# Loading only the non-zero halves of a filter's tables, with interleaved columns, for the first batch

## The chip, the cores and the metric

The kernel runs on one core of a Trainium2 chip. The metric is device time in microseconds, the median of several runs. The engines are named as in the profile: PE (TensorE matmul), PEld (its weight loads), DVE (VectorE), ACT (ScalarE), POOL (GpSimd) and SP (SyncE, which here only issues DMAs).

## The reference

Eight batches of 3008 x 256 float32 go through a spectral filter along the sequence (an FFT, a product with a complex filter, an inverse FFT), and the result through an MLP mixer over tokens and channels.

```python
X = np.fft.rfft(x, axis=1)                       # x: (8, 3008, 256)
Y = X * (filt_r + 1j * filt_i)[None]             # filters: (1505, 256)
x = np.fft.irfft(Y, n=3008, axis=1).astype(np.float32)

h = np.maximum(x.transpose(0, 2, 1) @ w_tok1, 0.0) @ w_tok2     # 3008 -> 256 -> 3008
u = x + h.transpose(0, 2, 1)
h2 = np.maximum(u @ w_ch1, 0.0) @ w_ch2                         # 256 -> 1536 -> 256
return (u + h2).astype(np.float32)
```

## The kernel before

The length 3008 is split as 47 x 64, and the Fourier transforms are written as matmuls with tables: first one of length 64 (`a_unit`), then one of length 47 (`b_unit`), the product with the filter on DVE, then the inverse of length 47 (`bi_unit`). The inverse of length 64 is folded into the mixer. The batches go through the filter in groups (0), (1, 2), (3, 4), (5, 6), (7). The first group, batch 0, has code of its own inside `dft` (`first` is true): its intermediate values stay on chip, transposed by DVE in the tile `turned`, and nothing else can run on PE but the conversion of the mixer's weights, which are stored in 64 bits and are rebuilt as float32 meanwhile. From the second group on, the filter's steps are slotted between the mixer's matmuls of earlier batches.

For the first batch the loop runs over k = 0 to 31. Step k does `b_unit(k)` (a matmul of 128x128 by 128x256 on L617, then a DVE product on L622) and `bi_unit(k - 1)` (two accumulating matmuls with 96 columns of weights on L631, then an ACT copy on L641). Two steps form a pair, which shares one table tile and one filter tile. Once a pair:

- `table_load` (L559) loads the table of the pair four ahead, by SP. It has the forward table (128 columns) and the inverse one (96 columns) for both steps of the pair: 128 rows of 2 x 224 floats. The tiles come from the pools `wbp` (three buffers) and `t1p` (two) in turn, so that five tables are on chip at once.
- `filt_load` (L225 to L232) loads the filter rows of the pair four ahead, by POOL, in six DMAs.
- `filt_double` (L237) and `table_turn` (L244, L245) copy on ACT: the filter's rows to the other half of the partitions, and the inverse table with its halves exchanged and one of them negated, into `turn_i`.
- the pair's results are written to DRAM by an ACT DMA (L638), and read back later into the `t4` tiles (L726).
- a tile of w_tok1 (by SP, L332) or w_tok2 (by POOL, L347) is loaded and converted (ACT L265, DVE L267 to L273, PE L311 and L312, ACT L314).

The tables have zeros. In the stored form their rows stand for four kinds of values; rows 0 to 63 reach only forward columns 0 to 63 and inverse columns 0 to 47, and rows 64 to 127 only the other columns. The kernel before loads the zeros too.

The order of the work on each engine is the order of the calls in the code (a manual schedule). Within a step of k the kernel calls `b_unit(k)`, then, on even k, `filt_load` and `table_load`, then `bi_unit(k - 1)`, and on odd k `filt_double` and `table_turn` for the next pair; the conversions follow at the end of the step. After the loop the first token sums (L732) start, and then the mixer.

Of the kernel before, what the change touches and what calls it, by code (L numbers as in the profile page):

```python
# [10 lines left out]
FP32 = mybir.dt.float32  # L11
# [12 lines left out]
P = 128  # L24
K2 = 32
A = 24
KR = 4 * A
KH = KR // 2
HALF = 64
# [5 lines left out]
XF = 2 * FB  # L35
KC = 2
WC = 2
DT = 256
TC = DT // P
DC = 1536  # L40
# [15 lines left out]
def _make_tables():  # L56
    n2 = np.arange(N2)
    one, two = slice(0, HALF), slice(HALF, P)
    wa = np.zeros((P, K2, 4))
    wai = np.zeros((K2, 4, P))  # L60
    for k2 in range(K2):
        th, th1 = (2 * np.pi * ((n * k2) % N2) / N2 for n in (n2, n2 + 1))
        c, s, c1, s1 = np.cos(th), np.sin(th), np.cos(th1), np.sin(th1)
        alt, alt1 = 1.0 - 2.0 * (n2 % 2), 2.0 * (n2 % 2) - 1.0
        rows = ((c, c1), (-s, s1), (-s, -s1), (c, -c1)) if k2 else ((c, c1), (alt, alt1), (c, -c1), (alt, -alt1))
        for g, (plus, minus) in enumerate(rows):
            wa[one, k2, g], wa[two, k2, g] = plus, minus
        wai[k2] = wa[:, k2].T * (2.0 if k2 else 1.0)
    wa, wai = wa.reshape(P, P), wai.reshape(P, P)

    n1 = A - 1 - np.arange(A)
    wb = np.zeros((4, A, K2, P))
    wi = np.zeros((P, K2, 4, A))
    for k2 in range(K2):
        for s in range(2 * A):
            if s < A:
                k, sign, q = k2 + 64 * s, 1.0, s
            else:
                j = s - A + 1
                k, sign, q = 64 * j - (k2 if k2 else 32), -1.0, 32 + s - A  # L80
                if j == A and k2:
                    continue
            th = 2 * np.pi * ((n1 * k) % N) / N
            c, sn = np.cos(th), np.sin(th)
            edge = k in (0, NF - 1)
            if edge:
                sn = np.zeros(A)
            if k2:
                parts = ((0, q, c), (1, q, sign * sn), (2, HALF + q, sign * c), (3, HALF + q, -sn))
            else:  # L90
                parts = ((s // A, q, c), (2 + s // A, HALF + q, -sn))
            for g, to, w in parts:
                wb[g, :, k2, to] = w * np.where(n1 == 0, 0.5, 1.0)
                wi[to, k2, g] = w * (1.0 if k2 or edge else 2.0) / N
    f = np.float32
    wi = wi.reshape(P, K2, KR)
    wa0 = wa.reshape(P, K2, 4).transpose(0, 2, 1).reshape(P, P)
    wbi0 = np.zeros((4, K2, K2, P + KR))
    wbi0[:, 0:A, :, 0:P] = wb
    wbi0 = wbi0.reshape(P, K2, P + KR)  # L100
    wbi0[:, :, P:] = wi
    wb = wb.reshape(KR, K2, P)
    wbi = np.zeros((P, K2 // KC, 4, HALF))
    for h in range(2):
        r, to = slice(h * HALF, h * HALF + KH), slice(h * HALF, (h + 1) * HALF)
        for i in range(KC):
            wbi[r, :, i] = wb[h * KH:(h + 1) * KH, i::KC, to]
            wbi[i * HALF:(i + 1) * HALF, :, 2 + h, 0:KH] = wi[to, i::KC, h * KH:(h + 1) * KH]
    wa = wa.reshape(P, K2, 4)
    by_sum = np.zeros((P, 2, 2, K2))  # L110
    for e in range(2):
        for h in range(2):
            by_sum[:, e, h, 0] = wa[:, 0, 2 * e + h]
            by_sum[:, e, h, 1:] = wa[:, 1:, 2 * h + e]
    wa = by_sum.reshape(P, P)
    return wa.astype(f), np.concatenate((wa[one], wa[one])).astype(f), wa0.astype(f), wai.astype(f), wbi.astype(f), wbi0.astype(f)
# [3 lines left out]
def kernel(  # L120
# [11 lines left out]
    nc = tc.nc  # L132
# [7 lines left out]
    wbi_d = nc.inline_tensor(wbi_np, name="wbi_t").ap()  # L140
    wa0_d = nc.inline_tensor(wa0_np, name="wa0_t").ap()
    wbi0_d = nc.inline_tensor(wbi0_np, name="wbi0_t").ap()
# [8 lines left out]
    def pool(name, bufs, **kw):  # L151
        return ctx.enter_context(tc.tile_pool(name=name, bufs=bufs, **kw))
# [3 lines left out]
    t1p = pool("t1p", 2)  # L156
    wbp = pool("wbp", 3)
# [15 lines left out]
    def bank(tag):  # L173
        return (psg if tag == "pg" else psum).tile([P, 512], FP32, tag=tag, name="ps_" + tag)
# [5 lines left out]
    def free_bank():  # L180
        turn.reverse()
        return turn[0]
# [10 lines left out]
    filts_0 = list(filts)  # L193
    w1 = glob.tile([P, A, DT], FP32, name="w1")

# [4 lines left out]
    turned = wcp.tile([P, K2 * D + P], FP32, tag="wc", name="turned")  # L200
    wa0 = turned[:, K2 * D:]
    turned = turned[:, 0:K2 * D].rearrange("p (s d) -> p s d", d=D)
# [32 lines left out]
    def filt_double(c):  # L235
        t = filts_0[c % len(filts_0)]
        nc.scalar.copy(out=t[HALF:P], in_=t[0:HALF])  # L237


    turn_i = sp.tile([P, 4, WC, KR], FP32, tag="s", name="turn_i")  # L240

    def table_turn(g, wb):
        wi, to = wb[:, :, P:], turn_i[:, g % 4]
        nc.scalar.copy(out=to[0:HALF], in_=wi[HALF:P])  # L244
        nc.scalar.activation(out=to[HALF:P], in_=wi[0:HALF], func=AF.Copy, scale=-1.0)  # L245

# [71 lines left out]
    def w1_load(i):  # L318
# [6 lines left out]
        for h in range(2):  # L325
# [3 lines left out]
            if h == 0:  # L329
                src = bass.AP(tensor=rows.tensor, offset=rows.offset + (A - 1 - lo) * DT,  # L330
                              ap=[[N1 * DT, N2], [-DT, n], [1, DT]])
            q.dma_start(st[h * HALF:(h + 1) * HALF, 0:n * DT].rearrange("p (a t) -> p a t", t=DT), src)  # L332
        yield
# [180 lines left out]
    def half_of(half, n=HALF):  # L514
        return slice(half * HALF, half * HALF + n)
# [30 lines left out]
    def dft(bs):  # L546
        first = bs[0] == 0
        nb = len(bs)
        tiled = bs not in GROUPS[0:2]
        todo = [(b, c) for b in bs for c in range(NXC // 2 if tiled else NXC)]  # L550
        wbs = {}

        def table_load(c):
            if c * KC % WC == 0:
                g = c * KC // WC
                where, tag = (t1p, "t1") if first and g % 5 > 2 else (wbp, "wb")
                shape, src = ([P, WC, P + KR], wbi0_d[:, ts(g, WC), :]) if first else ([P, 4, HALF], wbi_d[:, g])
                wbs[g] = where.tile(shape, FP32, tag=tag, name="wb")
                nc.sync.dma_start(wbs[g], src)  # L559

        def w_load(c):
            table_load(c)
# [51 lines left out]

        def b_unit(k):
            ps = bank("pg").rearrange("p (b d) -> p b d", b=2)[:, 0:nb, :]
            nc.tensor.matmul(ps, wbs[k // WC][:, k % WC, 0:P], turned[:, k, :].unsqueeze(1), start=True, stop=True)  # L617
            t = filts_0[k // KC % len(filts_0)]
            if k == 0:
                prods["all"] = p1p.tile([P, 2, 2, D], FP32, tag="p1", name="p1")  # L620
            p1 = prods["all"][:, k % 2]
            nc.vector.tensor_tensor(out=p1, in0=ps.to_broadcast([P, 2, D]), in1=t[:, :, k % KC, :], op=ALU.mult)  # L622
            prods[k] = (p1[:, 0:1], p1[:, 1:2])

        def bi_unit(k):


            ps = bank(free_bank()).rearrange("p (b d) -> p b d", b=2)[:, 0:nb, :]
            for i, p in enumerate(prods.pop(k)):
                wi = turn_i[:, k // WC % 4, k % WC] if i else wbs[k // WC][:, k % WC, P:]  # L630
                nc.tensor.matmul(ps[0:KR], wi, p, start=(i == 0), stop=(i == 1))  # L631
            c, r = divmod(k, KC)
            if r == 0:
                where, tag = (p2p, "p2") if c % 3 == 2 else (t3p, "t3")
                t3s[c] = where.tile([KR, KC, nb, D], FP32, tag=tag, name="t3")
            by_block(t3s[c][:, r], ps[0:KR])
            if r == KC - 1:
                nc.scalar.dma_start(g_d[0][ts(c, KC)].rearrange("k r b d -> r k b d"), t3s.pop(c))  # L638

        def by_block(out, ps):  # L640
            nc.scalar.copy(out=out.rearrange("p b (e g i) -> p b g e i", e=DH, i=CW),  # L641
                           in_=ps.rearrange("p b (g e i) -> p b g e i", e=DH, i=CW))
# [52 lines left out]
        if first:  # L695
            for i in range(2):
                t = t2p.tile([P, 2, KC, D], FP32, tag="t2", name="filt")
# [6 lines left out]
        for k in range(K2 + 1):  # L704
            if k < K2:
                b_unit(k)
                if first and k % KC == 0:
                    if k // KC + 4 < K2 // KC:
                        filt_load(k // KC + 4)
                    if k // KC + 4 < K2 // KC:  # L710
                        table_load(k // KC + 4)
            if k >= 1:
                bi_unit(k - 1)
            if first and k % KC == KC - 1 and k + 1 < K2:
                filt_double(k // KC + 1)
                table_turn(k // KC + 1, wbs[k // KC + 1])
            yield
# [338 lines left out]
    with tc.manual_schedule():  # L1056
# [6 lines left out]
        for i, _ in enumerate(dft(GROUPS[0])):  # L1063
            if i == 0:
                nc.scalar.dma_start(wai_t, wait_d)
            k = i - NXC - 2
# [113 lines left out]
```

## Time and profile before

| | |
|---|---|
| time, median of 3 runs | 2464.59 us (2463.82 to 2464.80) |
| the profiled execution's own time | 2465.54 us |
| its span, first to last instruction | 2463.4 us |
| PE busy | 2414.3 us, 98% of the span |
| DVE, ACT, POOL busy | 75%, 28%, 24% |
| DMA | 236.07 MB, of which 16 table loads of 224 KB for the first batch |
| loop over k of the first batch | 31.28 to 109.55 us of the span |
| granted clock of PE, mean | 0.994 |

All times inside the execution are counted from the start of the span. In a line of instructions in order of time, the first number is the start, the second the time taken (for several instructions, from the first start to the last end), and what stands in brackets is the idle time before it and what ended that. In a line of waits, the numbers are the total, how many times, and the longest.

### The profile page before, as it was taken

The numbers are of one execution on the slowest core, as the hardware profiler recorded it, in microseconds if no ns is written. First come the engines' busy times: TensorE is split into PE (matmuls) and PEld (weight loads), VectorE is DVE, ScalarE is ACT, GpSimd is POOL, SyncE is SP. The second block draws the span as 40 slices with busy tenths as digits, with TensorE's granted clock in tenths as the row PEclk, the third lists the DMA queues.
The fourth block names the chain that finished last, engine by engine and source line by source line (L and its number), as shares of the span: only waits on it lengthen the run. The fifth ranks groups of instructions, "written<-read, shape, count | busy, mean of one in ns | idle before, by whom it ended". The sixth has DMA issues, their size and how long they took to land.

```text
span 2463.4 us, 33933 instructions
## 1 busy us (share of the span) xinstructions
PE 2414.3 (98%) x11836; PEld 1962.0 (80%) x11836; DVE 1843.2 (75%) x3404; ACT 679.4 (28%) x1348; POOL 594.1 (24%) x1081
## 2 busy tenths in 40 slices
PE   7899999999999999999999999999999999999998
PEld 3566676978878887887888878897888888898887
DVE  7787778587885888578875887857786788757776
ACT  5633222133221222123221222213221222212222
POOL 6573332112111211211221112112212112112121
PEclk8999999999999999999999999999999999999999
DMA  9974434353431321235332322323322121201100
GB/s 214 254 223 134 140 112 139 103 156 115 119 88 49 86 84 56 90 109 167 101 84 69 86 73 79 103 57 116 98 66 73 50 71 46 97 24 29 40 14 20
DMA packets 173586, 236.07 MB, mean 96 GB/s; under 512 B 33757, under 2 KB 123563, under 8 KB 173416
## 3 DMA queue, kind: packets, MB, share of 16 engines
q1 hardware_dynamic: 128600, 175.59, 24.3%
q0 software_dynamic: 33216, 48.32, 7.9%
q10 hardware_dynamic: 11600, 10.00, 1.3%
q8 instruction: 94, 1.54, 0.3%
q14 instruction: 76, 0.62, 0.1%
HBM read 156.56 MB, written 77.22 MB: 95 GB/s over the span
## 4 chain that ended last, share of the span: by engine, by line
PE 88%; DVE 7%; DMA 2%; issue 1%; ACT 1%; POOL 0%; DVEq 0%; SPq 0%; ACTq 0%; POOLq 0%
PE ps_po L889 33%; PE ps_pg L855 18%; PE ps_pg L871 14%; PE ps_b L732 3%; PE ps_acc L732 3%; PE ps_b L512 3%; PE ps_b L776 3%; PE ps_acc L776 2%; PE ps_acc L512 2%; PE ps_b L754 2%; PE ps_acc L754 2%; DVE t L833 1%; DVE hh L833 1%; DMA filt<-in_filt_i_dram 1%; DVE u L833 1%
## 5 line engine op out<-in xcount | busy, mean ns | idle before, releaser
L936 POOL DMA_DIRECT2D out_dram<-r x752 | 408.1, 551 | 1645.3 <-ACT hh L876 1467.3
L833 DVE TENSOR_TENSOR hh<-ps_pg,s 128x512 f32<-128x512 f32 (+3 forms) x864 | 482.6, 586 | 383.9 <-ACT s L858 379.7
L876 ACT ACTIVATE hh<-hh 128x512 f32<-128x512 f32 (+1 forms) x576 | 348.0, 621 | 958.4 <-DVE hh L833 956.4
L889 PE MATMUL ps_po<-t,wc 128*128 128x256 f32 (+1 forms) x2304 | 546.4, 380 | 4.6 <-DVE t L833 3.5
L889 PEld LDWEIGHTS ps_po<-t,wc 128*128 128x128 f32 x2304 | 426.6, 190 | 129.5 <-DVE t L833 43.0
L889 PE MATMUL ps_po<-hh,wc 128*128 128x256 f32 (+1 forms) x1728 | 414.2, 375 | 1.3 <-POOL wc L371 0.8
L855 PE MATMUL ps_pg<-v,wc 128*128 128x256 f32 (+1 forms) x1728 | 414.7, 376 | 0.0
L889 PEld LDWEIGHTS ps_po<-hh,wc 128*128 128x128 f32 x1728 | 326.8, 190 | 42.9 <-ACT s L858 3.9
L855 PEld LDWEIGHTS ps_pg<-v,wc 128*128 128x128 f32 x1728 | 327.7, 190 | 40.4 <-DVE v L833 2.6
L871 PE MATMUL ps_pg<-u,wc 128*128 128x256 f32 (+1 forms) x1152 | 295.1, 379 | 0.5 <-DVE hh L833 0.5
L871 PEld LDWEIGHTS ps_pg<-u,wc 128*128 128x128 f32 x1152 | 215.0, 190 | 57.1 <-DVE hh L833 23.5
L833 DVE TENSOR_TENSOR t<-t,hh 128x256 f32<-128x256 f32 (+1 forms) x576 | 245.0, 425 | 19.9
L833 DVE TENSOR_TENSOR s<-ps_pg,hh 128x512 f32<-128x512 f32 (+1 forms) x288 | 196.1, 681 | 31.4 <-DVE hh L833 1.8
L858 ACT COPY s<-ps_pg 128x256 f32<-128x256 f32 (+1 forms) x288 | 106.0, 368 | 331.4 <-PE ps_pg L855 328.4
L833 DVE TENSOR_TENSOR t<-hh 128x512 f32<-128x512 f32 (+1 forms) x288 | 193.2, 671 | 0.6 <-ACT hh L876 0.6
L855 PE MATMUL ps_pg<-u,wc 128*128 128x256 f32 (+1 forms) x576 | 171.7, 380 | 2.6 <-DVE hh L833 2.6
L871 PE MATMUL ps_pg<-v,wc 128*128 128x256 f32 (+1 forms) x576 | 168.8, 375 | 0.0
L855 PEld LDWEIGHTS ps_pg<-u,wc 128*128 128x128 f32 x576 | 106.8, 190 | 34.3 <-DVE hh L833 18.9
L871 PEld LDWEIGHTS ps_pg<-v,wc 128*128 128x128 f32 x576 | 109.2, 190 | 12.6
L833 DVE TENSOR_TENSOR u<-ps_b,u 128x256 f32<-128x256 f32 (+2 forms) x102 | 58.3, 572 | 67.3 <-PE ps_b L776 61.8
L833 DVE TENSOR_TENSOR u<-ps_acc,u 128x512 f32<-128x512 f32 (+2 forms) x108 | 62.4, 577 | 55.8 <-PE ps_acc L776 51.5
L732 PE MATMUL ps_b<-t,w 128*128 128x256 f32 x384 | 86.3, 388 | 4.0 <-issue 4.0
(134 smaller groups left out, 2460.3 us busy)
## 6 DMA issues: line engine op xcount, KB each, us to landing
w<-w_tmp SPq DMA_DIRECT2D x35, 896.0 KB
out_dram<-r POOLq DMA_DIRECT2D x696, 32.0 KB, 2.4
t<-g_tmp SPq DMA_DIRECT2D x42, 512.0 KB
g_tmp<-t SPq DMA_DIRECT2D x96, 192.0 KB
t<-z_tmp SPq DMA_DIRECT2D x180, 96.0 KB
z_tmp<-t SPq DMA_DIRECT2D x60, 256.0 KB
filt<-in_x_dram SPq DMA_DIRECT2D x90, 128.0 KB
wb<-wbi_t SPq DMA_DIRECT2D x64, 128.0 KB
```

What stands on the lines that cost most here:

```text
L512: nc.tensor.matmul(outs(i, j), stat(i, j), mov(i, j), start=True, stop=True)
L732: nc.tensor.matmul(acc[:, t, :], w1[:, a, ts(t, P)], t4[b, a // TC4][:, a % TC4, :], start=(a == 0 and t == 0), stop=(a == A - 1 and t == ...
L754: nc.tensor.matmul(ps[:, ds(q * P, n)], t4[b, c][:, r, ts(dh, P)], wai[:, 0:n], start=(first and q == 0), stop=(not first and q == 3))
L776: nc.tensor.matmul(ps[:, ds(j * hw, hw)], h1[:, n, :], w2m[m % 2][:, at, 0:hw], start=(i < 2 and j == 0), stop=(j == len(todo) - 1))
L833: nc.vector.tensor_tensor(out=out, in0=in0, in1=in1, op=op)
L855: nc.tensor.matmul(ps[:, 0:hw], chan[0][:, jp, n, :], mov, start=True, stop=True)
L858: nc.scalar.copy(out=s[:, 0], in_=g[0][:, 0, 0:hw])
L871: nc.tensor.matmul(ps[:, 0:hw], chan[0][:, jp, n, :], mov, start=True, stop=True)
L876: nc.scalar.activation(out=hs, in_=hs, func=AF.Relu)
L889: nc.tensor.matmul(po[i][:, j, 0:hw], chan[1][:, jp, n, :], mov, start=(jp == 0 and first == 1), stop=(jp == JP - 1 and last == 1))
L936: q.dma_start(bass.AP(tensor=ob.tensor, offset=ob.offset + row * D + g * cw, ap=[[N1 * D, 32], [D if h else -D, n], [1, cw]]), blocks[ts(g ...
```

## The change

For the first batch, each half of the partitions now gets only its own half of the columns. To make each of these a single contiguous run, the columns are stored in another order: forward and inverse columns alternate, and so do the two steps of the pair, so that a column's next neighbour is four elements away. A tile is now 256 places by 2 steps; rows 0 to 63 take the first 128 places, rows 64 to 127 the last 128, each by a DMA of its own. The other half of each tile must be zero. So the first five tables allocate five tiles that are kept for the whole loop, and POOL clears the half that is never loaded once in each (two memsets of 64x256 a tile, ten in all, of which one is for each half). The matmuls and `table_turn` read the columns with a step. The call of `table_load` moves behind `bi_unit(k - 1)`, since the kept tile that it writes is read there for the last time. The later groups load their tables as before.

```diff
+TI = P - 2 * KH + 1
...
+    places = np.zeros((P, K2, 2 * P))
+    places[:, :, 0::2] = wbi0[:, :, 0:P]
+    places[:, :, TI:TI + 2 * KR:2] = wbi0[:, :, P:]
+    wbi0 = np.concatenate((places[one, :, 0:P], places[two, :, P:]))
+    wbi0 = wbi0.reshape(P, K2 // WC, WC, P).transpose(0, 1, 3, 2)
...
     def table_turn(g, wb):
-        wi, to = wb[:, :, P:], turn_i[:, g % 4]
+        wi, to = wb[:, TI:TI + 2 * KR:2].rearrange("p r k -> p k r"), turn_i[:, g % 4]
...
+        kept = []
 
         def table_load(c):
-            if c * KC % WC == 0:
-                g = c * KC // WC
-                where, tag = (t1p, "t1") if first and g % 5 > 2 else (wbp, "wb")
-                shape, src = ([P, WC, P + KR], wbi0_d[:, ts(g, WC), :]) if first else ([P, 4, HALF], wbi_d[:, g])
-                wbs[g] = where.tile(shape, FP32, tag=tag, name="wb")
-                nc.sync.dma_start(wbs[g], src)
+            if first:
+                if c < 5:
+                    where, tag = (t1p, "t1") if c > 2 else (wbp, "wb")
+                    t = where.tile([P, 2 * P, WC], FP32, tag=tag, name="wb")
+                    for h in range(2):
+                        nc.gpsimd.memset(t[half_of(h), ts(1 - h, P)], 0.0)
+                    kept.append(t)
+                wbs[c] = kept[c % 5]
+                for h in range(2):
+                    nc.sync.dma_start(wbs[c][half_of(h), ts(h, P)], wbi0_d[half_of(h), c])
+            else:
+                wbs[c] = wbp.tile([P, 4, HALF], FP32, tag="wb", name="wb")
+                nc.sync.dma_start(wbs[c], wbi_d[:, c])
...
-            nc.tensor.matmul(ps, wbs[k // WC][:, k % WC, 0:P], turned[:, k, :].unsqueeze(1), start=True, stop=True)
+            nc.tensor.matmul(ps, wbs[k // WC][:, 0:2 * P:2, k % WC], turned[:, k, :].unsqueeze(1), start=True, stop=True)
...
-                wi = turn_i[:, k // WC % 4, k % WC] if i else wbs[k // WC][:, k % WC, P:]
+                wi = turn_i[:, k // WC % 4, k % WC] if i else wbs[k // WC][:, TI:TI + 2 * KR:2, k % WC]
...
                 if first and k % KC == 0:
                     if k // KC + 4 < K2 // KC:
                         filt_load(k // KC + 4)
-                    if k // KC + 4 < K2 // KC:
-                        table_load(k // KC + 4)
             if k >= 1:
                 bi_unit(k - 1)
+            if first and k % KC == 0 and k // KC + 4 < K2 // KC:
+                table_load(k // KC + 4)
```

## The prediction

> **What bounds the kernel now.** I read the page's slices first: PE is busy 98% of the 2463.4 us span, and only the first two of the 40 slices fall below nine tenths. The change touches the first batch's filter alone, so I asked for busy time by stretch, then for who waited for whom inside it (31 to 110 us), then for the instructions in order of time.
>
> ```profile
> 31.00:51.00 20.00, 19.72 (x67) 12.72 (x68) 13.94 (x25) 13.68 (x26) 10.71 (x20) 0.91 1.06 206
> 51.00:73.00 22.00, 20.78 (x76) 12.55 (x75) 16.60 (x30) 17.05 (x36) 14.81 (x27) 1.00 1.05 257
> 73.00:91.00 18.00, 18.00 (x67) 11.60 (x66) 13.74 (x25) 14.12 (x28) 12.45 (x23) 1.00 0.97 251
> 91.00:113.00 22.00, 17.34 (x57) 9.20 (x56) 14.13 (x28) 14.07 (x31) 7.64 (x15) 1.00 0.84 259
> ```
>
> The columns are length, busy PE, weight loads, DVE, ACT, POOL, then clock, DMA share and GB/s. The reader is to see a PE nearly full and DMA engines that are full (0.97 to 1.06) for the first three stretches.
>
> ```profile
> 42.25 0.59 PE L617 MATMUL ps_pg<-turned,wb 128*128 128x256 f32 x2
> 46.56 0.59 PE L617 MATMUL ps_pg<-turned,wb 128*128 128x256 f32 x2
> 92.19 0.59 PE L617 MATMUL ps_pg<-turned,wb 128*128 128x256 f32 x2
> 94.24 0.67 PE L631 MATMUL ps_b<-p,wb 128*96 128x256 f32 x2 [1.45 <-DVE p L622]
> ```
>
> One pair of k (one table) takes 46.56 - 42.25 = 4.31 us where nothing is late: that is PE's floor. From 31.28 to 109.55 the 16 pairs took 78.3 us; 16 x 4.31 = 69.0, so 9.3 us are waits. By the starts of the pairs' first matmuls they sit in: the first pair 2.4 (a cold start), the pair at 50.87 1.1, at 64.90 to 74.94 1.4, at 92.19 2.7, and 1.7 in the last two. What they wait for:
>
> ```profile
> ACT t L641 <- DMA g_tmp<-t: 1.8, 1, 1.8
> ACT w L314 <- DMA wb<-wbi_t: 1.3, 1, 1.3
> DVE p L622 <- DMA filt<-in_filt_r_dram: 9.7, 8, 2.5
> DVE p L622 <- ACT filt L237: 8.9, 6, 2.9
> SPq L559 <- DMA g_tmp<-t: 8.7, 2, 6.4
> POOL filt L232 <- DMA filt<-in_filt_r_dram: 6.7, 9, 1.3
> ```
>
> All are transfers landing late: filter rows, the results' write-out, a table. The fifth line shows a coupling: in the trace every DMA issued from SP and ACT raises one of eight semaphores taken in turn, and waits until that semaphore's earlier transfer has landed.
>
> ```profile
> 53.78 0.37 ACT L641 COPY t<-ps_b 96x256 f32<-96x256 f32 x1
> 55.24 0.35 ACT L244 COPY turn_i<-wb 64x192 f32<-64x192 f32 x1
> 55.60 0.36 ACT L245 ACTIVATE turn_i<-wb 64x192 f32<-64x192 f32 x1
> 57.83 0.37 ACT L641 COPY t<-ps_b 96x256 f32<-96x256 f32 x1
> ```
>
> ACT, back to back, needs 57.83 - 53.78 = 4.05 us a pair: only 0.26 us under PE's floor. Anything added to ACT beyond that sets the pace.
>
> **Part 1, fewer bytes.** A table load shrinks from 128 rows of 1792 B to two DMAs of 64 rows of 1024 B: 229,376 to 131,072 B, 1.57 MB over 16 tables. In the trace's packet records a 1792 B packet took 111 ns on average between 31 and 110 us, and one of 1024 B on that queue 88 ns in the start-up; scaling 111 by bytes gives 64 ns. I take 72, between them but nearer to the scaled one, since the 4096 B packets (272 ns) lie on the same line. Saved: 39 ns x 2048 packets / 16 engines = 5.0 us of DMA time, 4.1 of it (13 of 16 tables) inside the loop; between the ends 2.9 and 6.0 over all.
>
> How much of this reaches PE? Only the waits can shrink. The one at 50.87 comes from the write-out issued at 38.30 and landed at 49.6, 11.3 us in a full queue: 98 kB less of the roughly 1,100 kB a pair (4.31 us at 257 GB/s), with smaller loads ahead of it, should take most of the 1.1 (take 0.9). Of the 1.4 between 64.90 and 74.94 take half, 0.7. At 92.19 the tables are all loaded (last issue 81.60) and POOL's filter loads are late for their own landing times: take 0.5 of 4.4. Sum -2.1; bounds 0 and -6.
>
> Here a rule speaks against the change. Row first: the weight tiles of w_tok1 (L332) are loaded by halves of 64 partitions already, 4096 B a row, and their packets move at the same rate per byte (272 / 4096 = 0.066 ns a byte against 111 / 1792 = 0.062). The Trainium skill, "SBUF — State Buffer", section "Can I just issue two DMAs to hit both halves?", says that a transfer on 64 partitions uses half the ports and that two of them serialize, gaining only 6% over one; its table gives 196 GB/s for 64 partitions and 328 for 128 (at 1 MiB). As an estimate from that page, 131 kB at 196 GB/s are 0.67 us and 229 kB at 328 are 0.70: nothing saved, and my -2.1 would be 0. In this stretch many transfers share the engines at 206 to 259 GB/s in all, so I go by the row and keep the rule for a rival.
>
> **Part 2, strided weight loads.** The columns are now 4 elements (16 B) apart. No weight load of the trace is strided. Rows near it:
>
> ```profile
> L858 ACT COPY s<-ps_pg 128x256 f32<-128x256 f32 x5 | 1.9, 372 | 2.2 <-ACT t L528 1.8 <-PE ps_pg L855 0.5
> L314 ACT COPY w<-ps_po 128x512 f32<-128x512 f32 x12 | 7.0, 586 | 7.2 <-PE ps_pg L617 2.3 <-PE ps_acc L631 1.9 <-DMA wb<-wbi_t 1.3
> L314 ACT COPY w<-ps_po 128x240 f32<-128x240 f32 x6 | 3.5, 581 | 3.2 <-PE ps_po L312 2.0 <-ACT t L641 0.8 <-PE ps_b L631 0.4
> 144.10 0.86 PEld L754 LDWEIGHTS ps_acc<-wai,t 128*128 128x128 f32 x7 [0.24 <-issue]
> ```
>
> Contiguous copies give (586 - 372) / 256 = 0.84 ns an element over a fixed 158 ns; the copy that writes with a stride gives (581 - 158) / 240 = 1.76, so a stride costs 0.92 ns an element. The last line shows seven loads of 190 ns each in 0.86 us: loads overlap, one every 0.11 us. The Trainium skill, "Advanced Engine Details and Errata", section "SBUF Cachelines", says that at least two hits on a 16-byte line are needed for full speed: at 16 B apart every column opens a new line, so the rule says that each load pays, but gives no figure. If the time for a column doubles, the rate is one load in about 0.22 us, and the matmul beside it starts every 0.215 us: hidden. I take that, plus 0.5 us for restarts after waits, where the load isn't covered. Counted instead as occupancy (190 + 107 = 297, 163 + 80 = 243 ns), 64 loads pay 82 ns and 64 pay 28: +7.0 us. Bounds 0 and +7; beyond that it is the rival.
>
> **Part 3, ACT's turn of the table.** L244 and L245 now read with that stride: 192 x 0.92 = 0.18 us each by the strided copy, 0.36 a pair. ACT's floor becomes 4.41, 0.10 above PE's: 16 x 0.10 = +1.6. Bounds: 0 (a strided read may be free where a strided write was not) and 16 x 0.36 = +5.8. I take +1.6.
>
> **Part 4, the move, the semaphores, the memsets.** table_load now stands after bi_unit(k - 1), past ACT's write-out but past no other SP or POOL issue. It has to wait for the reader of the buffer's last table, which it did before (SP waited 5.8 us for PE's L631 there), and its table is used four pairs, some 17 us, later: nothing. SP issues 16 more DMAs of 0.33 us, 0.33 a pair, while it waits for landings more than that: nothing, and +5 if SP ran behind. But five DMAs a pair in place of four now share the eight semaphores, so each must land within 1.6 pairs (6.9 us) instead of 2 (8.6). They are smaller, so I book nothing; 0 to +4. PE waits for two landings in place of one at each table: 16 x 0.05 (the "issue" gaps of the chain) = 0.8 at most, take 0.3. Ten memsets of 64x256: the memset of 64x1024 took 0.97 us and the one of 64x512 0.52, so 0.28 each. Six stand before the filter loads of 22.10 us, 1.7 us; the POOL queue behind them waited 1.2 us for landings up to 26.6, and 0.5 at 30.36, which covers them. The pair for the fifth buffer falls into POOL's wait of 0.72 at 35.69. Nothing; +2 without that cover. Padding in SBUF: none.
>
> **Sum.** -2.1 + 0.5 + 1.6 + 0.3 = +0.3 us. The profiled execution took 2465.54 us (2463.4 of span and 2.1 around it), 0.95 above the median of 2464.59; so 2465.8 by it and 2464.9 by the median. I say 2465.0. The stages after the loop follow its end (token sums at 117.90 wait for the last write-outs), so that a microsecond here is about one in the total.
>
> **Rivals.** *Faster: the loop is bound by DMA throughput.* For it: shares of 0.97 to 1.06, and every late operand is a transfer. Then the whole 5.0 to 6.5 us (1.57 MB at 231 GB/s is 6.8) come off, if ACT's strided reads are free: 2459. Against it: next to no wait of PE in 75 to 92, though the DMA is as full there. *Slower: the strided weight load is slower than the matmul beside it.* Place: L617 and the first L631 of each step. It decides from 0.215 us a load on; at 297 ns PE pays 7.0 us, in pairs that have no slack. With ACT's 1.6 and 0.3, less 2.0 of smaller waits: 2464.6 + 7 = about 2472. Were the recorded 190 and 163 doubled, 64 x 165 + 64 x 111 ns = 17.7, near 2480. For it: no such load in the trace, and the rule of lines. *The halves cost as much as the whole* (the port rule): -2.1 goes, 2467, within the same class. That the change doesn't do what it says is excluded for the bytes, not for the time.
>
> **Chances.** A measurement of this kernel can tell about 0.2%, 4.9 us. Near balance (with the port rival) 0.56, DMA-bound gain 0.19, slow weight loads 0.25 (some of it the semaphores' turn). The range runs from 2458, the gain's far end, to 2473, past the slow loads' centre; what is left out is mostly the doubled loads.
>
> **What would show it.** The table's packets shorter, DMA share of 51 to 73 below 1.05; PEld of L617 still about 190 or up to 300 ns, with L617 pairs still 4.3 us apart; L244 and L245 at 0.53 us; no new wait of POOL before 22 us. I am wrong if undelayed pairs are over 4.6 us apart (PE or ACT bound), or if the loop ends before 106 us.

## The result, and the profile after

The changed kernel takes 2458.86 us (2455.28 to 2462.23, 10 runs) against 2463.57 for the kernel before beside it (10 runs). The ratio is 0.998 with a 95% interval of 0.997 to 0.9989: it is faster by 4.7 us, a little under 0.2%, and the interval leaves no change out. The forecast had been 2465.0 with "no change" as the likeliest class, so it was wrong; the time is that of its rival "bound by DMA throughput" (2459), though not for that rival's reason, as the runs below show.

The profiled execution took 2459.61 us, with a span of 2457.5. Lines have moved in the code: `b_unit`'s matmul is L631 now (was L617), its DVE product L636 (L622), `bi_unit`'s matmuls L645 (L631), ACT's turn L250 and L251 (L244, L245), the table's DMA L570 (L559), its memset L566, the token sums L746 (L732). The same stretches as before, with the same columns (length, busy PE, weight loads, DVE, ACT and POOL, clock, DMA share, GB/s):

```profile
31.00:51.00 20.00, 20.00 (x65) 14.17 (x66) 14.40 (x26) 14.07 (x25) 16.16 (x31) 0.87 0.93 207
51.00:73.00 22.00, 22.00 (x82) 16.61 (x81) 16.90 (x30) 19.58 (x36) 18.43 (x34) 1.00 1.02 272
73.00:91.00 18.00, 18.00 (x67) 13.58 (x67) 13.72 (x26) 16.09 (x29) 10.69 (x20) 1.00 0.98 240
91.00:113.00 22.00, 19.19 (x61) 12.37 (x61) 17.60 (x39) 15.46 (x33) 4.82 (x10) 0.96 0.87 217
```

PE is full in the first three stretches, although DMA is still close to full in two of them: the transfers now land in time. In order of time, one pair on PE and one on ACT:

```profile
42.74 0.61 PE L631 MATMUL ps_pg<-turned,wb 128*128 128x256 f32 x2
47.09 0.61 PE L631 MATMUL ps_pg<-turned,wb 128*128 128x256 f32 x2
...
48.77 0.37 ACT L655 COPY t<-ps_b 96x256 f32<-96x256 f32 x1
50.24 0.54 ACT L250 COPY turn_i<-wb 64x192 f32<-64x192 f32 x1
50.81 0.57 ACT L251 ACTIVATE turn_i<-wb 64x192 f32<-64x192 f32 x1
53.21 0.37 ACT L655 COPY t<-ps_b 96x256 f32<-96x256 f32 x1
```

A pair takes 47.09 - 42.74 = 4.35 us on PE (4.31 before) and 53.21 - 48.77 = 4.44 on ACT. After the second pair (4.99), every pair lies between 4.21 and 4.48; before, seven were 4.66 to 6.02. The waits inside the loop (total, times, longest), those that answer to the ones of before:

```profile
DVE p L636 <- ACT filt L243: 8.3, 8, 1.4
DVE p L636 <- DMA filt<-in_filt_i_dram: 3.7, 4, 1.0
POOL filt L238 <- DMA filt<-in_filt_r_dram: 0.9, 2, 0.7
DVE p L636 <- DMA filt<-in_filt_r_dram: 0.6, 1, 0.6
PE ps_acc L645 <- DVE p L636: 0.5, 1, 0.5
```

DVE's wait for filter rows went from 9.7 to 0.6 us (and 3.7 on the other filter, none long), POOL's from 6.7 to 0.9, and ACT's waits for a write-out and for a table are not in the list any more. What lands sooner is seen in the list of DMA issues from 0 to 110 us (engine, count, size, median us from issue to landing), first of the kernel before, then of the changed one:

```profile
filt<-in_filt_r_dram POOLq DMA_DIRECT2D x15, 48.0 KB, 7.1
```

```profile
filt<-in_filt_r_dram POOLq DMA_DIRECT2D x15, 48.0 KB, 4.7
```

The change doesn't touch these transfers. They come through POOL's queue and share the DMA engines with the tables, and they land 2.4 us sooner.

**Where the 5.94 us between the two spans (2463.41 and 2457.47) went.** By landmarks on PE: the loop's first matmul comes 0.46 us earlier (31.28, 30.82). From there to the matmul that the prediction took as the loop's end (109.55; now at 104.49) it is 78.27 against 73.67, -4.60. From there to the first token sum it is 8.35 against 6.06, -2.29. The token sums up to the next step (L762 before, L776 after) take 24.38 against 23.33, -1.05. The mixer takes 2314.0 against 2316.5, +2.45. Nothing of the change is in the mixer; over these two and the eleven profiles below its length goes from 2313.6 to 2316.6 in no order of the tables, so I count that as scatter; single spans that differ by 2 us or so tell nothing. (The medians differ by 4.7 and these two executions by 5.9: the one of before was 2.0 above its median, the one of after 0.75.)

The stretch behind the loop was in my sum only as following the loop one for one. What PE waits for there is the results' read-back (`t4`). SP issues a read-back when the write-out that it needs has landed. In the kernel before (PE's waits for semaphores at L732: shortest, median and longest in ns; then, in order of time, SP from 105 us on and PE):

```profile
L732 PEldq EVENT_SEMAPHORE  x3: 51/51/5005, 112.8 to 118.1; - x3
...
110.35 4.02 SPq L726 DMA_DIRECT2D t<-g_tmp  x9
...
117.90 1.62 PE L732 MATMUL ps_b<-t,w 128*128 128x256 f32 x3 [3.98 <-issue]
```

The last line says only "issue", but the semaphore records tell more. A write-out issued at 100.94 lands at 110.28, after 9.3 us; the last nine of SP's read-backs are all issued behind it, and PE's wait of 5.0 us ends when the one issued at 113.08 has landed, at 117.81. In the changed kernel the write-out of the same pair (issued at 96.81) lands after 4.1 us, at 100.91. Six of the nine read-backs go out from there on, and three are left for the time after the last write-out:

```profile
108.16 1.23 SPq L740 DMA_DIRECT2D t<-g_tmp  x3
...
110.55 1.90 PE L746 MATMUL ps_b<-t,w 128*128 128x256 f32 x5 [1.92 <-DMA t<-g_tmp]
```

The token sums are shorter because of the clock. Stretches of 5 us (length, busy PE, granted clock, DMA share, GB/s), before and then after:

```profile
110.00:115.00 5.00, 3.13 (x8) 1.00 0.76 165
115.00:120.00 5.00, 2.10 (x5) 0.66 0.99 208
120.00:125.00 5.00, 5.00 (x16) 0.66 1.04 339
125.00:130.00 5.00, 5.00 (x25) 1.00 0.66 171
```

```profile
105.00:110.00 5.00, 3.26 (x8) 1.00 0.52 109
110.00:115.00 5.00, 4.45 (x13) 0.66 1.05 220
115.00:120.00 5.00, 5.00 (x25) 1.00 1.02 347
```

Before, the clock was 0.66 in two stretches, up to 125 us; after, in one. This part is at least partly chance: over the 13 traces the sums take 21.6 to 24.4 us, the trace of before has the longest, and in a second trace of the changed kernel (the last but one below) no stretch fell below 1.00 and they took 22.0.

### The profile page after: what moved, and what is told of

Same layout as the page of the kernel before. It is cut to its first block, busy times and chain, and to the rows that moved or that the text cites. A ratio compares the mean times of both kernels' runs of the same rounds, so it can differ in the third digit from the quotient of the medians.

```text
span 2457.5 us, 33961 instructions
## 1 busy us (share of the span) xinstructions
PE 2413.4 (98%) x11836; PEld 1967.7 (80%) x11836; DVE 1845.0 (75%) x3404; ACT 685.1 (28%) x1348; POOL 601.5 (24%) x1091
## 4 chain that ended last, share of the span: by engine, by line
PE 88%; DVE 6%; DMA 3%; issue 1%; ACT 1%; POOL 0%; DVEq 0%; ACTq 0%; SPq 0%; POOLq 0%
PE ps_po L903 33%; PE ps_pg L869 18%; PE ps_pg L885 14%; PE ps_b L746 3%; PE ps_acc L746 3%; PE ps_b L518 3%; PE ps_b L790 3%; PE ps_acc L790 2%; PE ps_acc L518 2%; PE ps_b L768 2%; PE ps_acc L768 2%; DVE t L847 1%; DVE hh L847 1%; DVE p L669 1%; DVE u L847 1%
## 5 line engine op out<-in xcount | busy, mean ns | idle before, releaser
L746 PE MATMUL ps_b<-t,w 128*128 128x256 f32 x384 | 85.3, 385 | 1.9 <-DMA t<-g_tmp 1.9
```

What stands on the lines that cost most here:

```text
L746: nc.tensor.matmul(acc[:, t, :], w1[:, a, ts(t, P)], t4[b, a // TC4][:, a % TC4, :], start=(a == 0 and t == 0), stop=(a == A - 1 and t == ...
```

## The experiments

Each run was measured beside the kernel before on the same chip: medians of it 2463.97 for the first four, 2462.90 for the next four, 2463.09 for the last three. The question was which part of the change brings the gain: the bytes that are not loaded, the cut into two DMAs, the move of the call, or fewer bytes in flight between issue and landing.

**Whole tables with everything else kept.** The interleaved layout, the kept buffers and the moved call stay, but the whole tile of 128 rows by 2048 B is loaded by one DMA (262 kB), and nothing is cleared.

```diff
...
-                    for h in range(2):
-                        nc.gpsimd.memset(t[half_of(h), ts(1 - h, P)], 0.0)
...
-                for h in range(2):
-                    nc.sync.dma_start(wbs[c][half_of(h), ts(h, P)], wbi0_d[half_of(h), c])
+                nc.sync.dma_start(wbs[c], wbi0_d[:, c])
```

> The changed kernel (kept tiles, moved load, interleaved columns with their step of 16 B), but each table is loaded whole by one DMA of 128 rows of 2048 B, zeros included, and nothing is cleared by POOL: 262 kB a table against 229 before and 131 in the changed kernel. Theory A (the gain is the DMA time of the bytes that are no longer moved): the gain is gone, pairs wait for transfers again, and with a little more traffic than before and the strided reads it takes 2464 to 2469 us, loop end at 108 us or later. Theory B (the gain is the later place of the load and the kept tiles, not the bytes): about 2459 us, loop end near 103 us.

Measured: 2466.20 us, ratio 1.0011 (1.0002 to 1.0019). The gain is gone, and a small loss is left. The filter rows land late again, and the waits are back (DMA issues, then waits):

```profile
filt<-in_filt_r_dram POOLq DMA_DIRECT2D x15, 48.0 KB, 7.0
...
POOL filt L237 <- DMA filt<-in_filt_r_dram: 11.1, 10, 2.9
```

Late pairs are back as well, but only at the end: the third to the twelfth take 4.35 to 4.47 us, the next three 5.86, 6.79 and 5.60. So the gain lies in how the tables are loaded, not in the layout, the buffers or the order.

**The cut alone.** The kernel before, with its whole 224 KB tables, each loaded by two DMAs of 64 rows.

```diff
-                nc.sync.dma_start(wbs[g], src)
+                if first:
+                    for h in range(2):
+                        nc.sync.dma_start(wbs[g][half_of(h)], src[half_of(h)])
+                else:
+                    nc.sync.dma_start(wbs[g], src)
```

> The kernel before, with each of the first batch's table loads cut in two DMAs of 64 rows of 1792 B: same bytes, twice the DMAs. Theory A (bytes): no gain, 2463 to 2466 us; a loss if five DMAs a pair in the turn of eight semaphores hurt. Theory B2 (what helps is that smaller transfers stand ahead of others in the turn of the semaphores): 2459 to 2461 us.

Measured: 2460.36 us, ratio 0.9987 (0.9979 to 0.9996). The same bytes in two pieces gain 3.6 us: I had allowed the fifth DMA of a pair 0 to +4. In its trace (DMA issues, waits, and stretches with the columns of the first fence):

```profile
filt<-in_filt_r_dram POOLq DMA_DIRECT2D x15, 48.0 KB, 6.0
...
ACT t L645 <- DMA g_tmp<-t: 4.4, 1, 4.4
...
31.00:51.00 20.00, 20.00 (x66) 12.83 (x66) 14.67 (x26) 14.03 (x28) 14.21 (x26) 0.87 1.05 236
51.00:73.00 22.00, 22.00 (x83) 14.37 (x82) 17.89 (x32) 18.71 (x37) 16.24 (x29) 1.00 1.03 249
73.00:91.00 18.00, 18.00 (x70) 11.91 (x69) 13.97 (x26) 14.44 (x29) 10.54 (x20) 1.00 1.05 262
...
95.00:105.00 10.00, 6.34 (x13) 4.01 (x14) 4.87 (x9) 6.86 (x14) 2.16 (x4) 0.66 0.95 264
```

The filter rows land 1.1 us sooner with not a byte less, and eleven pairs in a row take 4.31 us, the floor, with DMA shares of 1.03 to 1.05. Then one write-out is 4.4 us late and the fifteenth pair takes 9.18, so in this profile the loop is not shorter in all (first to last matmul of the loop 77.1 us, 76.5 before). Its gain is seen behind the loop, where the token sums start at 115.92 (117.90 before) and take 21.6 us (24.4): the low clock came at the late pair, where PE waited anyway. That the cut gains is shown by the medians; in which stretch it does so is known from one execution only.

**The move alone.**

```diff
-                    if k // KC + 4 < K2 // KC:
-                        table_load(k // KC + 4)
             if k >= 1:
                 bi_unit(k - 1)
+            if first and k % KC == 0 and k // KC + 4 < K2 // KC:
+                table_load(k // KC + 4)
```

> The kernel before with nothing but the call of table_load moved behind bi_unit(k - 1). Theory A (bytes): no change, 2463 to 2465 us. Theory B (order): most of the gain, 2459 to 2461 us.

Measured: 2464.56 us, ratio 1.0003 (0.9994 to 1.0011). No difference, as booked.

**A step of two elements in place of four.** Forward and inverse columns alternate, but the two steps of a pair lie one behind the other. The bytes are the same, in rows of 2 x 512 B.

```diff
-    wbi0 = wbi0.reshape(P, K2 // WC, WC, P).transpose(0, 1, 3, 2)
+    wbi0 = wbi0.reshape(P, K2 // WC, WC, P)
...
-            nc.tensor.matmul(ps, wbs[k // WC][:, 0:2 * P:2, k % WC], ...
+            nc.tensor.matmul(ps, wbs[k // WC][:, k % WC, 0:2 * P:2], ...
...
```

> The changed kernel with only forward and inverse columns alternating, the two steps kept apart: same bytes as the changed kernel, but 256 packets of 512 B a table in place of 128 of 1024 B, and a column step of 8 B in place of 16. Weight loads of the tables should fall from 309 ns back to about 190 if a step of 8 B is free. Theory A in its form of bytes: 2458 to 2459 us; in its form of packet time (512 B packets took 39 to 52 ns, so some 11 us of all engines' time over 256 x 16 packets divided by 16, against 14 before and 7.6 to 9.6 in the changed kernel): about half of the gain, 2461 us.

Measured: 2457.59 us, ratio 0.9974 (0.9964 to 0.9984). The loss that was expected from the number of packets (2461) did not come. The single instructions (min, median and max in ns), first of the changed kernel and then of this one:

```profile
L631 PEld LDWEIGHTS ps_pg<-turned,wb x64: 307/309/337, 30.8 to 99.8; 128*128 128x128 f32 x64
L250 ACT COPY turn_i<-wb x16: 536/540/546, 29.8 to 99.5; 64x192 f32<-64x192 f32 x16
```

```profile
L631 PEld LDWEIGHTS ps_pg<-turned,wb x64: 195/196/337, 30.7 to 99.9; 128*128 128x128 f32 x64
L250 ACT COPY turn_i<-wb x16: 359/364/379, 29.4 to 99.3; 64x192 f32<-64x192 f32 x16
```

The cost of the stride is almost gone, and the pairs are back at 4.31 us (the fifteenth, 5.56, is late). That is 16 x 0.04 = 0.6 us of PE, and some 0.25 more by ACT (below): that is all that the traces show of what the step of four costs.

**A useless DMA behind each table.** The kernel before, with a DMA of 2 kB (128 rows of 16 B into a spare tile) issued behind each table load of the first batch: a fifth turn of the eight semaphores, with next to no bytes.

```diff
...
                 nc.sync.dma_start(wbs[g], src)
+                if first:
+                    nc.sync.dma_start(scratch[:, g], ident_d[:, 0:4])
```

> The kernel before, with one useless DMA of 2 kB (128 rows of 16 B into a tile that nothing reads) issued by SP behind each of the 16 table loads. Same useful bytes, one more place taken in the turn of eight semaphores: of the transfers of SP and ACT at most 8 are in flight, in kB 8 x 928 / 4 = 1856 before and 8 x 930 / 5 = 1488 now (the splitting of the table load has the same 1485). Theory C (what counts is how many bytes SP and ACT have in flight, since the filter rows on POOL's queue land behind them): POOL's filter loads land in about 5.8 us in place of 6.4 to 7.1, and 2459.5 to 2462 us. Theory A (bytes moved only): no change, 2463 to 2465 us.

Measured: 2467.01 us, ratio 1.0014 (1.0005 to 1.0022): slower. The filter rows land after 6.5 us, hardly sooner. So it is not the fifth turn as such that helps.

**Another load cut smaller.** The kernel before, with each load of w_tok1 made in two DMAs of half as many rows (128 kB).

```diff
-            q.dma_start(st[h * HALF:(h + 1) * HALF, 0:n * DT].rearrange("p (a t) -> p a t", t=DT), src)
+            to = st[h * HALF:(h + 1) * HALF, 0:n * DT].rearrange("p (a t) -> p a t", t=DT)
+            for r in (slice(0, HALF // 2), slice(HALF // 2, HALF)):
+                q.dma_start(to[r], src[r])
```

> The kernel before, with the table loads as they were, but each of the w_tok1 loads of 256 kB cut in two by partitions (four DMAs of 32 rows a tile). Same bytes, six DMAs a pair in place of four, 8 x 928 / 6 = 1237 kB in flight. Theory C: filter loads land in 4.5 to 5.3 us and most of the changed kernel's gain is there without a byte less: 2457 to 2461 us. Theory A: no change or a loss by more issues, 2463 to 2466 us.

Measured: 2466.61 us, ratio 1.0013 (1.0005 to 1.0022): slower. The DMA issues, the waits (SP's too), and a stretch with the columns of the first fence:

```profile
filt<-in_filt_r_dram POOLq DMA_DIRECT2D x15, 48.0 KB, 4.2
...
PE ps_pg L619 <- DMA wb<-wbi_t: 3.3, 2, 2.7
...
SPq L334 <- DMA g_tmp<-t: 18.6, 6, 5.7
...
31.00:51.00 20.00, 20.00 (x66) 12.83 (x66) 14.70 (x26) 14.10 (x29) 12.94 (x24) 0.87 0.76 199
```

The filter rows land sooner than in the changed kernel, and the time is worse. On the line of w_tok1 SP waits 18.6 us for write-outs that hold the next semaphores (0.4 in the kernel before), and the DMA engines have a share of 0.76 in the first stretch where the kernel before had 1.06. PE loses nothing there yet, but later tables are late, and it waits 3.3 us for them. The theory that fewer bytes in flight are better, without more, falls with this run: here so few are under way that the DMA engines are idle while SP waits.

**No tables but the first five.** The changed kernel, loading only those.

```diff
-                for h in range(2):
+                for h in range(2 if c < 5 else 0):
```

> The changed kernel with only the first five tables loaded; the later pairs read one of those five again, so that the tables' traffic inside the loop is gone (the products of pairs 5 to 15 are with other tables' values). 0.7 MB less than the changed kernel, but three DMAs a pair of 235 kB, up to 1877 kB in flight. Theory A: at least as good as the changed kernel, 2456 to 2459 us, filter landing at or below 4.7 us. Theory C in its strict form: filter landing back at 6 us or more while w_tok1 is loaded, 2460 us or more.

Measured: 2456.20 us, ratio 0.9975 (0.9965 to 0.9984). Taking away all the bytes of the eleven other tables brings 0.0005 to 0.0008 of the time more than halving them did (0.998 and, below, 0.9983), 1 to 2 us, and the intervals overlap: little is left to gain there. The pairs stay at 4.35, the floor of PE with the strided loads, up to the twelfth; the last three that can be told are 4.45, 5.00 and 4.71. The filter rows land after 4.8 us, no sooner than in the changed kernel, and not after 6 us or more, as the count of bytes in flight would have it: the three DMAs a pair are on the average as large as the four of the kernel before (235 and 232 kB).

**Step of two, and w_tok1 cut.** The kernel of the step of two elements with the edit of w_tok1's loads.

> The kernel with a column step of 8 B and the cut w_tok1 loads together: fewest bytes in flight (8 x 832 / 7 = 951 kB), weight loads at full rate. The loop's pairs are at PE's floor of 4.31 us in the first already, so that little is left in the loop: 2455 to 2458 us. If SP's issues (seven a pair at 0.33 to 0.6 us) fall behind, 2459 or more.

Measured: 2462.82 us, ratio 1.0002 (0.9994 to 1.0011). The gain is lost: DMA share 0.68 in the stretch from 31 to 51 us, and the loop's last matmul at 107.23 again. PE waits 2.6 us for late tables: it is the shortage of the run with w_tok1 cut, with the tables made smaller still.

**Whole tables in two pieces.** As in the first experiment, but the 262 kB in two DMAs of 64 rows. Against the first it changes the pieces, against the changed kernel the bytes.

```diff
-                nc.sync.dma_start(wbs[c], wbi0_d[:, c])
+                for h in range(2):
+                    nc.sync.dma_start(wbs[c][half_of(h)], wbi0_d[half_of(h), c])
```

> The changed kernel with whole tables loaded (262 kB each, zeros included, nothing cleared by POOL), but by two DMAs of 64 rows, as many as in the changed kernel. Against the run with one DMA of 128 rows (2466.2 us) it has the same bytes in two pieces; against the changed kernel it has the same pieces with twice the bytes. If the bytes decide: 2463 to 2467 us, waits in the loop, filter loads landing in 6 us or more. If the two pieces decide: 2459 to 2461 us, filter loads at 5 to 5.5 us.

Measured: 2463.36 us, ratio 0.9999 (0.999 to 1.0008). Two pieces in place of one: 2466.20 to 2463.36 (on other chips, with intervals that overlap). Half the bytes in two pieces: 2463.36 to 2459.71 (next run, same chip). The two intervals against the kernel before just meet; taken directly, the difference is 3.65 us, with a 95% interval of about 0.7 to 6.4 by drawing anew from the eleven times of each. The trace (DMA issues, then SP and PE in order of time) shows where the bytes count in this execution:

```profile
filt<-in_filt_r_dram POOLq DMA_DIRECT2D x15, 48.0 KB, 5.9
...
108.98 4.01 SPq L737 DMA_DIRECT2D t<-g_tmp  x9
...
116.36 2.90 PE L743 MATMUL ps_b<-t,w 128*128 128x256 f32 x6 [5.02 <-DMA t<-g_tmp]
```

In two pieces the loop runs at 4.35 us a pair even with whole tables, up to the fifteenth (5.72), and its last matmul starts at 103.23, near that of the changed kernel (102.70). But the token sums start at 116.36 and not at 110.55. The write-out issued at 97.31 lands only at 108.91, after 11.6 us, and as in the kernel before the last nine of SP's read-backs are issued behind it. So the backlog that the bytes make is paid behind the loop here.

**The changed kernel and the step of two again,** side by side with the last.

> The changed kernel itself, again, on the same chip as the next one. All theories: 2457 to 2460 us.

> The kernel with a column step of 8 B again, beside the changed kernel. The step of 16 B costs PE 0.04 us a pair (4.35 against 4.31), 0.7 us in all, and ACT some 0.37 us a pair that it has to spare: 0 to 2 us under the changed kernel, which the interval may not tell.

Measured: 2459.71 us, ratio 0.9983 (0.9974 to 0.9991), and 2458.38, ratio 0.9975 (0.9964 to 0.9985). Both gains hold on another chip. The step of two elements is 1.3 us below the step of four, side by side; the intervals overlap, so that the medians alone don't show it, but the rows of the weight loads and of the pairs do (0.04 us a pair). It beats the kernel before on both chips and has the lowest medians of the versions here that load all the tables.

## Why the prediction was wrong

**The forecast fell at two terms: the fewer bytes (-2.1, with the stages after the loop following one for one), and the fifth DMA (nothing, 0 to +4).** *The loop.* The wait at 50.87 was to give 0.9 of its 1.1, and it went. Of the waits between 64.90 and 74.94 I took half; all went. At 92.19 I gave 0.5 because the tables are all loaded by then; the late pairs there (6.02 and 5.78, counted by the even steps where the prediction's list has the odd ones) now take 4.21 and 4.48. The loop gave 4.60 with the stride's cost inside, so some 5.2 of the 9.3 us of waits; I had booked 2.1. It is not the bytes alone that did this: in the cut alone, with not a byte less, the pairs are on the floor too until the fifteenth, and even with whole tables in one piece the new layout holds 4.35 to 4.47 us up to the twelfth. Which part of the change ended which wait in the loop stays open. *The stretch behind the loop* gave a further 2.29, through the read-backs, and, by the clock and partly by chance, 1.05. Here the bytes do separate the kernels. In the five traces with half tables (or none after the fifth) and uncut loads of w_tok1, the token sums start between 109.50 and 111.37; in the other eight, between 115.63 and 118.90.

What I had missed, as far as the traces tell, is that lateness is carried on: POOL's filter and w_tok2 loads stand in one queue, and a late landing holds the issues behind it. In the kernel before, five tiles of w_tok2 were issued between 99.48 and 103.11, around the write-out that then took 9.3 us; in the changed kernel five went out one by one between 85.05 and 98.58. That these tiles made the write-out late fits, but no run tests it.

**The cut.** I had priced two DMAs by what they cost (a turn more of the semaphores) and not by what they do to others' transfers. The cut of whole tables gains 3.6 us by itself (2463.97 to 2460.36), so the sign was wrong. Why it gains stays open. An explanation that fits is that eight transfers may be under way from SP and ACT (in the traces their DMAs raise eight semaphores between them), and smaller ones put fewer bytes ahead of POOL's rows: 7.1 us to landing in one piece, 6.0 in two, 4.7 in two halves. It is not the whole story. The useless DMA also makes the mean transfer smaller, and it lost 3 to 4 us, with rows landing after 6.5; without the later tables it is no smaller than in the kernel before, and the rows land after 4.8. Nor do landing times alone rank the kernels: with w_tok1 cut they are 4.2 us and time is lost, because SP waits for its next semaphore (share 0.76). Half the bytes in a single DMA was not run.

**How the two add up** can't be split to the microsecond. With tables in one piece, the changed layout gave 1.0011; in two pieces 0.9999; in two halves 0.998 and 0.9983. By medians the first of these steps is worth 3 us and the second 4 to 5. They don't add up to the gain over the kernel before, since the changed layout with its larger whole tables starts 0.0011 above it. Whether the cut and the bytes take away the same waits is not shown.

**Right:** the stride. Weight loads of 128 columns take 309 ns (297 forecast by the occupied time) and of 96 columns 260 (243). As I chose, they hide beside the matmuls: a pair is 0.04 us longer, 0.6 in all against 0.5. The rival of slow weight loads (+7.0) did not come. The rule of the Trainium skill ("Advanced Engine Details and Errata", "SBUF Cachelines") agrees with both steps that were run: with a step of 8 B a 16-byte line is hit twice and the load takes 196 ns; with 16 B it is hit once and the load pays. The 0.3 for waiting for two landings at each table was not paid: with the step of four a pair takes 4.35 us with one DMA a table and with two. SP's issues were taken too small (0.33 us; in the changed kernel each takes 0.52), without a cost that shows on PE.

**Right in size, not paid:** ACT's turn takes 0.54 and 0.56 us (0.53 forecast), and ACT's pair was to be 4.41 and is: from the 42nd microsecond on, eleven pairs in a row are 4.37 to 4.47 apart by the starts of L250. But the sum had 16 x 0.10 = +1.6 for PE, as if ACT's pace were PE's at once. ACT began with room: it falls behind PE by 0.07 us a pair, some 0.7 in ten pairs, before PE sees it. Only the tenth to the thirteenth pair show it (4.38, 4.41, 4.40, 4.48), about 0.25 us in all. The second trace of the changed kernel has the same from the eleventh on (4.38, 4.43, 4.49), and the step of two, where ACT's copies are short, stays at 4.31.

**The memsets** take 0.31 us each (0.28 forecast), but their cover was not where I put it. The changed kernel's instructions in order of time on POOL:

```profile
20.08 2.06 POOL L566 MEMSET wb<- 64x256 f32 x6
...
23.99 0.53 POOL L231 DMA_DIRECT2D filt<-in_filt_r_dram  x1
```

The filter loads that stood at 22.10 come at 23.99, 1.9 us later. My sign "no new wait of POOL before 22 us" was therefore the wrong one: it is no wait, it is a delay of issues. PE didn't pay for it at the loop's start (first matmul 0.46 us earlier); the second pair took 4.99 us where the kernel before had 4.31, and it is 4.85 with whole tables and no memsets, 5.29 with the cut alone, and 4.35 in the second trace of the changed kernel itself, so the memsets don't explain it.

**The port rule** (nothing saved by halves on 64 partitions) was given as a rival and didn't come: the tables' packets of 1024 B took 59.6 ns each on the average between 31 and 106 us (72 taken, 111 for 1792 B before), which is 5.4 us of the 16 engines' time (4.1 taken for the loop). Loads on 64 partitions did gain here; whether halves in other circumstances serialize no run here shows.

**The DMA-bound rival** had the time (2459) by another way: it took 5.0 to 6.5 us of transfers straight off the loop. In fact the DMA share fell in the first stretch (1.06 to 0.93) but stayed at 1.02 and 0.98 in the next two, where PE's waits went all the same; the cut alone has PE full in all three at 1.03 to 1.05 and with the same bytes. And with no more tables after the fifth the gain is hardly larger. So throughput isn't the measure of it.

## What to carry to other kernels

Where several queues share full DMA engines, price a transfer by what lands behind it: look up the landing times of the other queues' loads and ask which waits they end, as far as the stage behind. A landing time tells nothing until such a wait is found. How many pieces a load has is a knob of its own where few transfers may be under way: smaller pieces let others land sooner here, until the issuing queue had to wait for its turn. A strided weight load costs little (here 0.04 us a pair) while loads can still start about as often as the matmuls beside them; prefer the smaller step all the same.

## What the runs showed of the hardware that was not expected

- A column step of 16 B makes a load of 128 columns of weights 309 ns in place of 190; a step of 8 B only 196. On ACT a copy of 64x192 takes 540 ns, 364 and 349 with steps of 16 B, 8 B and none. I had thought of the step as one price.
- Late in the loop or behind it, where PE was short of work, the granted clock fell to 0.66 for 5 to 10 us in several traces and was still there when PE was full again (120 to 125 us in the kernel before). Where that hits the token sums they take 23.3 us (changed kernel) or 24.4 (before), and 21.6 where it came earlier (the cut alone). It doesn't follow each gap: in the second run of the step of two, PE was busy for 2.13 of 5 us before the token sums, the clock stayed at 1.00, and they took 21.65 us.
- The useless DMA, 32 kB in sixteen issues, costs 0.14% (0.05 to 0.22). Its packets take 11 ns each between 31 and 110 us, 1.2 us of the 16 engines' time, less than the 3.4 us lost. Why it costs as much stays open.
